# Sparse attention followed by a two-layer feed-forward: paced late loads, one more block in the seven-product form, and a re-ordered head

## Chip, cores and metric

The kernel runs on one core of a Trainium2 chip. The metric is device time in microseconds (us) of one execution; the median of three runs of the kernel before is 305.44 us (305.16 to 306.75).

## What is computed

```python
B, H, S, D = 8, 8, 576, 64
scores = q @ k.transpose / 8
mask_local   = (0 <= i - j) & (i - j < 32)          # heads 0 to 3
mask_strided = (i >= j) & (i % 32 == j % 32)        # heads 4 to 7
attn = softmax(where(mask, scores, -1e9)) @ v
x = attn laid out as [4608 tokens, 512]
h = x @ w_in                                        # 512 -> 2048
g = s * relu(h)**2 + b
out = g @ w_out                                     # 2048 -> 512, float32
```

## The kernel before, in words

Everything is in fp16 with fp32 sums. The attention of a batch is four pairs of heads: two local pairs (tiles of 96 queries against 128 keys) and two strided pairs (72 positions, 8 groups). A pair is a list of small TensorE steps: transposes of q and k, scores (L557), attention times v (L614, with a column of ones in v that gives the softmax sum), and transposes of the normalised result x (L662) into xT, where tokens lie along the free axis. For later batches the transposes of q, k and x are done by the DMA engines instead (`k_dma`, `q_dma`, `x_dma`, `x_out` with `x_in`), from the batch numbers in `QB_DMA, KB_DMA, QS_DMA, XS_DMA = 6, 4, 3, 4` on. The strided x of the last batch (7) is still transposed on TensorE.

The feed-forward runs over nine blocks T of 512 tokens. F1 (L907) makes 16 hidden tiles of 128 x 512, each of four matmuls of 512 columns; ScalarE or VectorE takes the relu, and a pair of tiles is then squared into gT. F2 multiplies gT by w_out. Blocks 0 to 2 do it plainly (`ff2`, L965): 4 token groups x 16 matmuls of 512 columns. From block `SEVEN = 3` on `ff2_seven` (L875) is used: the 2 x 2 split of the product with seven half-size products instead of eight, 112 matmuls of 256 columns. For it VectorE forms sums of the left operand (L747, eight instructions of 128 x 1024 a block) and combinations `w_mix` of the weights (L769, four instructions once, after F2 of block 2), and combines the results (L794, L806, L817) where the plain form has four evictions (L976).

The order of all instructions is written by a planner inside the kernel (`Plan`), at build time. It keeps an estimated clock, a free time for each engine and an estimated time at which each value is ready (`LAT` for latency after a queue's work, `landing(...)` and the table `AT` for loads), and emits TensorE's steps one by one: attention steps when they are ready and the attention is behind its due share (`due`), F1 and F2 steps otherwise, and filler matmuls (`keep_running`, L1201) where the first 16 F1 steps have not begun and nothing is ready. The estimates decide the order alone. On the chip each engine takes its instructions in that order and waits on semaphores, so a step that stands too early holds up all that stands behind it.

Loads of q, k, v and of the weights are issued on GpSimd's queue (POOL; the loads convert to fp16 on the way). For batch b + 2 they come in two bunches: `fetch_qk`, behind copies `gate` (L1036) that wait for the k transposes of the batch before, and `fetch_v`. From batch 4 on that is some 17 DMAs in a row. Local v of batch 0 is staged as fp32 in the space of w_out, in two halves, by SP's queue (`stage_v`, L252), and cast by GpSimd (L338). Stores of the output and all DMA transposes go through SP's queue.

At the start (the head) the order on GpSimd's queue is: q and k of batch 0, strided v, casts of v, the three loads of w_in behind a `gate` on qs (L1096), casts again, then the `second` bunch: q, k, v of batch 1 (four DMAs for local v, L316) and the four quarters of w_out (L334). AT and `landing` hold the planner's times for these.

Of the kernel before, what the change touches and what calls it, by code (L numbers as in the profile page):

```python
# [15 lines left out]
class Plan:  # L16
# [6 lines left out]

    LAT = {"A": 70.0, "V": 70.0, "P": 70.0, "D": 12000.0, "X": 7000.0, "Y": 12000.0}

# [3 lines left out]
    def __init__(self):  # L29
        self.t = 0.0  # L30
        self.done = {}
        self.pend = []
        self.free = {"A": 0.0, "V": 0.0, "P": 7000.0, "D": 0.0, "X": 0.0, "Y": 0.0}
        self.banks = {}
# [82 lines left out]
class Step:  # L117
    def __init__(self, fn, ns, needs=(), group=None, keys=(), posts=(), after=None):
        self.fn, self.ns, self.needs, self.group = fn, ns, needs, group
        self.keys, self.posts, self.after = keys, posts, after  # L120


@with_exitstack
def kernel(
# [32 lines left out]
    for p in range(SQ):  # L157
        for c in range(SQ):
# [29 lines left out]
    w_in_sb = [const.tile([128, 4, n], FP16, name=f"w_in_sb{i}")  # L188
               for i, n in enumerate((512, 512, 1024))]
    w_out_sb = const.tile([128, NFT, DM], FP16)  # L190
# [20 lines left out]
    def x_free(b):  # L211
# [21 lines left out]
    NL, NS = 4 * LT * D, 4 * ST * D  # L233
    vl_stage = w_out_sb.rearrange("p f m -> p (f m)").bitcast(FP32)[:, 0:NL].rearrange(
        "p (h t d) -> p h t d", h=4, d=D)

# [33 lines left out]
    for tl in p_bufs[False]:  # L270
        nc.vector.memset(tl[:, 16 * SQ:], 0.0)

    nc.vector.memset(part32, 1.0 / 32)
# [39 lines left out]
    def load_vl(b):  # L313
        vl = v_loc[b % NV]
        for h in range(4):
            nc.gpsimd.dma_start(out=vl[LPAD:128, h, :, 0:D], in_=v_band(b, h))  # L316
# [8 lines left out]
    def load_w_in():  # L325
        wv = moe_w_in.rearrange("(c p) f -> p c f", p=128)
        for i, at in enumerate((0, 512, 1024)):
            nc.gpsimd.dma_start(out=w_in_sb[i], in_=wv[:, :, at:at + w_in_sb[i].shape[2]])
# [26 lines left out]
    def cast_v(b, loc, mm, key):  # L355
        nt, np_, dst = (LT, 128, v_loc) if loc else (ST, SQ, v_str)

        def g(eng):
            src = vl_stage if loc else loaded[b, "vs"].rearrange(
                "p (h t d) -> p h t d", h=4, d=D)  # L360
            for h in range(2 * mm, 2 * mm + 2):
                copy_on(eng, out=dst[b % NV][0:np_, h, :, 0:D], in_=src[:, h])
        n = nt * D
        plan.post([key], {"P": 1000.0} if loc else {"A": 2 * (170 + 0.83 * n), "V": 540.0,
                                                           **({"P": 1500.0} if b == 0 else {})}, g,
                  [("cast", b, mm) if loc else ("in", "vs", b, mm)])
        if loc:
            rows_before(b, mm, ("cast", b, mm))

    def rows_before(b, mm, key):  # L370

        hs = slice(2 * mm, 2 * mm + 2)
        vl = v_loc[b % NV]
        src = vl_stage[:, :, :, 0:D] if b == 0 else vl[:, :, :, 0:D]

        def g(eng):
            copy_on(eng, out=vl[0:LPAD, hs, 1:LT, 0:D], in_=src[128 - LPAD:128, hs, 0:LT - 1])
        plan.post([key], {"P": 800.0} if b == 0 else {"A": 700.0, "V": 350.0}, g, [("in", "vl", b, mm)])

# [29 lines left out]
    def pair_steps(b, m):  # L409
# [10 lines left out]
        def trans(name, j, group):  # L420
            alone = loc and b < HEAD_T

            def f():
                if j == 0:
                    st["p" + name] = bank(group).bitcast(FP16)[:, 0:S]
                if alone:
                    for e in range(2):
# [11 lines left out]
                    rhs=ident[0:nq, 0:nq], is_transpose=True)  # L439
            s = Step(f, 70 if alone else 35, needs=[("in", name + sfx, b, mm)],  # L440
                     group=group if j == 0 else None)
            if j == nt - 1:
                key = ("t", name, id_)
# [33 lines left out]
        q_by_dma = b >= (QB_DMA if loc else QS_DMA)  # L477
        x_by_dma = b >= 2 if loc else XS_DMA <= b < B - 1

# [234 lines left out]
    SQ_ACT = 0  # L714
    SEVEN = 3
    H = NFT // 2
# [44 lines left out]
    def mix_post():  # L761

        wl, wr = [[w_out_sb[:, H * j:H * j + H, 256 * k:256 * k + 256] for j in range(2)]
                  for k in range(2)]
        jobs = ((3, wr[1], wr[0]), (1, wr[0], wl[0]), (2, wr[1], w_mix[1]), (4, wl[1], w_mix[2]))
        before = [("F2", SEVEN - 1)]
        for i, x, y in jobs:
            plan.post(before, {"V": 1250.0},
                      lambda eng, i=i, x=x, y=y: nc.vector.tensor_tensor(  # L769
                          out=w_mix[i], in0=x, in1=y, op=ALU.subtract), [("w_mix", i)])  # L770
            before = [("w_mix", i)]
        plan.post([("ev", SEVEN - 1, ts) for ts in range(4)], {"V": 350.0},
                  lambda eng: nc.vector.tensor_tensor(
                      out=bcs[:, 256:512], in0=bcs[:, 256:512], in1=bcs[:, 0:256],
                      op=ALU.subtract), [("dbc",)])
# [121 lines left out]
    def ff1(T, ft, ct, group, cts=(0, 1, 2, 3), early=False):  # L897
        tok0 = T * PS
        def f():
# [6 lines left out]
            for lo, hi in ((0, n), (n, PS))[:1 + (n < PS)]:  # L906
                nc.tensor.matmul(  # L907
                    out=gts["h", T, ft][:, lo:hi],
                    lhsT=w_in_sb[min(ft // 4, 2)][:, ct].rearrange(
                        "p (c x l) -> p c l x", x=128, l=4)[:, max(ft // 4 - 2, 0), ft % 4],  # L910
                    rhs=xT[ct][:, (at + lo) % (NX * S):(at + lo) % (NX * S) + hi - lo],
                    start=(ct == cts[0] and lo == 0), stop=(ct == cts[-1] and hi == PS))
# [109 lines left out]
    def landing(cost):  # L1022

        nonlocal ring
        ring = max(ring, plan.t + 2000.0) + cost

        return ring + (6000.0 if plan.t > 60000.0 else 600.0)

# [3 lines left out]
    def fetch_qk(b):  # L1032
# [6 lines left out]
        for name in ("q", "k"):  # L1039
# [3 lines left out]
            if b < HEAD_T:  # L1043
                arrive(both(name + "l", b), landing(1500))
                continue
            plan.done["raw", name, b] = landing(1700 if b > 1 else 1450)
            for mm in range(2):
                pair_post(b, name, mm, ("raw", name, b))
        for name in ("qs", "ks"):
            arrive(both(name, b), landing(2000 if b > 1 else 1750))  # L1050

# [11 lines left out]
    def early_v(b):  # L1063

        loaded[b, "vs"] = inp.tile([SQ, NS], FP16, tag="vs", name="vs")
        load_s(loaded[b, "vs"], v, b)
        plan.done["raw", "v", False, b] = landing(1800)
        for mm in range(2):
            cast_v(b, False, mm, ("raw", "v", False, b))

    gate = const.tile([64, 4], FP16)

    def after_landing(i, src):

        nc.sync.dma_start(out=gate[0:1, i:i + 1], in_=src)

    load_qk(0)
    early_v(0)
    plan.free["P"] = 7100.0
    plan.free["V"] = 6500.0  # L1080
    AT = {"ql0": 5700.0, "kl0": 6800.0, "ql1": 7900.0, "kl1": 8900.0, "qs": 10100.0,
          "ks": 11600.0, "vs": 13600.0, "vl0": 7100.0, "vl1": 14700.0}
    for key, at in AT.items():
# [4 lines left out]
    after_landing(0, loaded[0, "ql"][0:1, NL // 2:NL // 2 + 1])  # L1088
    stage_v(range(2, 4))
    nc.sync.dma_start(out=masks, in_=h_mask.ap())  # L1090
    nc.sync.dma_start(out=s_sb, in_=moe_s.to_broadcast([128, 1]))
    nc.sync.dma_start(out=b_sb, in_=moe_b.to_broadcast([128, 1]))
    def weights_in(eng):

        nonlocal ring
        nc.gpsimd.tensor_copy(out=gate[0:8, 2:3], in_=loaded[0, "qs"][64:SQ, 0:1])  # L1096
        load_w_in()
        ring = 15300.0
        for keys, cost in ([0], 2700), ([1], 2500), ([2, 3], 5000):
            arrive([("w_in", c) for c in keys], landing(cost))  # L1100

    for mm, at in (0, AT["vl0"]), (1, AT["vl1"]):
        plan.done["raw", "v", True, 0, mm] = at
        cast_v(0, True, mm, ("raw", "v", True, 0, mm))
    plan.post([("in", "vl", 0, 0)] + both("qs", 0), {"P": 2500.0}, weights_in, [("w",)])
# [6 lines left out]
    def second(eng):  # L1112

        fetch_qk(1)
        load_vl(1)
        plan.done["raw", "vl", 1] = landing(3200)
        for mm in range(2):
# [3 lines left out]

    plan.post(both("vl", 0) + both("vs", 0) + [("w",)], {"P": 14000.0}, second, [("free",)])

# [11 lines left out]
    for b in range(B):  # L1135
        for m in range(4):
            steps, last_av = pair_steps(b, m)
            att.append(steps)
            if b + 2 < B:

                if m == 0:
                    plan.post(
                        [("fetch_v", b + 1) if b else ("free",)] +
                        [("q", (b, mk)) for mk in range(4)] + [("k", (b, mk)) for mk in range(4)] +
                        [("soon" if b > 1 else "k", (b + 1 if b > 1 else b, mk)) for mk in range(2, 4)],
                        {"P": 2900.0 + (2200.0 if b + 2 >= QB_DMA else 0.0)},
                        lambda eng, b=b: fetch_qk(b + 2), [("fetch", b + 2)])
                last_av.after = when_all("av", b, lambda b=b: plan.post(
                    [("fetch", b + 2)] + both("vs", b), {"P": 3600.0}, lambda eng: fetch_v(b + 2),
                    [("fetch_v", b + 2)]))  # L1150

    f1, f2 = [], []
    for T in range(NBLK):
# [26 lines left out]
        for ts in range(4):  # L1180

            parts = 2 if T == NBLK - 1 and ts == 3 else 1
            for part in range(parts):
                gr = Group("f2", F2B)
                for ft in range(NFT):
                    f2.append(ff2(T, ts, ft, gr, part, parts))
                    f2[-1].pos = T + 0.25 + (ts + (part + ft / NFT) / parts) / 4
    def keep_running(until):

        ghz = 1.2 if plan.t < 6000 else 2.4  # L1190
        n = min(int((until - 100.0 - plan.t) * ghz) - 20, 512) // 128
# [25 lines left out]
    while i2 < len(f2) or any(at_i[p] < len(att[p]) for p in range(len(att))):  # L1217
# [4 lines left out]

        active = [p for p in range(first, min(first + 4, len(att))) if at_i[p] < len(att[p])]
        for p in active:
            r = plan.step_ready(att[p][at_i[p]])
# [66 lines left out]
```

## Time and profile before

| | |
|---|---|
| median of 3 runs | 305.44 us |
| the profiled execution, its own time | 306.2 us |
| its span, first to last instruction | 304.4 us |
| TensorE (PE) busy, first matmul, start of the last matmul | 296.4 us, 1.05 us, 300.97 us |
| VectorE (DVE), ScalarE (ACT), GpSimd (POOL) busy | 216.6, 183.9, 99.3 us |
| granted TensorE clock | 1.000 |
| q0, GpSimd's DMA queue | 57232 packets, 18.08 MB |
| q1, SP's DMA queue | 43562 packets, 18.78 MB |

A busy PE is not a PE at its peak: the ends of pipelined matmuls are modelled, so a matmul of 512 columns is listed with 379 ns while the next one starts some 216 ns after it. The pace is therefore read from pieces of the chain of work (so many matmuls in so many microseconds), not from the mean of one. In the waits, the columns are the total, the number of times and the longest, in microseconds. A GpSimd DMA row gives the time of the issuing instruction; its landing comes later.

### The profile page before, as it was taken

How to read it: one execution, taken by the hardware profiler on the slowest of the kernel's cores; microseconds unless marked ns; L12 is line 12 of the kernel's file. 1: busy time of each engine (PE TensorE's matmuls, PEld its weight loads, DVE VectorE, ACT ScalarE, POOL GpSimd, SP SyncE). 2: the span in 40 equal slices, each digit the busy share in tenths (PEclk: the TensorE clock that was granted, in tenths of full speed). 3: DMA queues.
4: the chain of work that ended last, by engine and by line, in shares of the span. 5: the costliest groups of instructions: out<-in, count | busy, mean ns of one | idle time of the engine just before them, and what ended most of it. 6: DMA issues, size and time to landing. Idle time of an engine off the chain costs nothing.

```text
span 304.4 us, 6800 instructions
## 1 busy us (share of the span) xinstructions
PE 296.4 (97%) x2674; PEld 205.8 (68%) x2674; DVE 216.6 (71%) x474; ACT 183.9 (60%) x330; POOL 99.3 (33%) x146
## 2 busy tenths in 40 slices
PE   8998999999999999999999999999999999999995
PEld 3764655666555568767567776778888666766784
DVE  6665897698966688737997698777765366737563
ACT  2966963898747677478585946695725445445300
POOL 8771753930961095029502961200000000000000
PEclk9999999999999999999999999999999999999999
DMA  8999999999999699999999999944010200300123
GB/s 136 183 201 202 137 213 190 179 198 149 83 160 165 98 100 149 132 186 147 142 153 172 142 160 159 155 105 131 14 37 34 72 34 0 106 0 2 69 82 126
DMA packets 100826, 37.29 MB, mean 122 GB/s; under 512 B 80907, under 2 KB 97803, under 8 KB 100795
## 3 DMA queue, kind: packets, MB, share of 16 engines
q0 software_dynamic: 57232, 18.08, 60.1%
q1 hardware_dynamic: 43562, 18.78, 33.3%
q8 instruction: 21, 0.34, 0.5%
q14 instruction: 11, 0.08, 0.1%
HBM read 36.86 MB, written 10.32 MB: 155 GB/s over the span
## 4 chain that ended last, share of the span: by engine, by line
PE 83%; DMA 8%; DVE 3%; POOL 3%; issue 1%; ACT 1%; POOLq 0%
PE ps_f L907 36%; PE ps_f L875 20%; PE ps_f L965 12%; DMA kl<-in_k_dram 5%; PE ps_s L557 3%; PE ps_a L614 3%; DMA vs<-in_v_dram 2%; PE ps_s L875 2%; DMA xT<-x_dram 1%; PE ps_t L875 1%; PE ps_s L965 1%; PE ps_t L614 1%; PE ps_t L662 1%; PE ps_t L437 1%; PE ps_f L437 1%
## 5 line engine op out<-in xcount | busy, mean ns | idle before, releaser
L907 PE MATMUL ps_f<-xT,w_in_sb 128*128 128x512 f16 (+4 forms) x696 | 148.1, 340 | 0.0
L934 ACT ACTIVATE u<-ps_f 128x512 f16<-128x512 f32 x137 | 80.8, 595 | 72.6 <-PE ps_f L907 69.9
L907 PEld LDWEIGHTS <-w_in_sb 128*128 128x128 f16 x704 | 71.7, 113 | 33.1 <-DMA w_in_sb<-in_moe_w_in_dram 0.5
L875 PEld LDWEIGHTS <-gT 128*128 128x128 f16 x512 | 49.0, 98 | 12.5 <-issue 0.4
L965 PE MATMUL ps_f<-w_out_sb,gT 128*128 128x512 f16 x176 | 47.6, 379 | 0.0
L875 PE MATMUL ps_f<-w_out_sb,gT 128*128 128x256 f16 x312 | 44.2, 273 | 0.3 <-DVE o L806 0.3
L944 DVE TENSOR_TENSOR gT<-u 128x1024 f16<-128x1024 f16 x46 | 32.1, 697 | 15.1 <-ACT u L934 14.4
L942 ACT ACTIVATE gT<-u 128x1024 f16<-128x1024 f16 x26 | 27.5, 1057 | 0.7
L640 DVE TENSOR_TENSOR x_nat<-ps_a,rec 72x256 f16<-72x256 f32 (+1 forms) x55 | 25.3, 459 | 0.9
L316 POOL DMA_DIRECT2D v_loc<-in_v_dram x28 | 20.7, 759 | 14.3 <-DMA w_in_sb<-in_moe_w_in_dram 6.0
L965 PEld LDWEIGHTS <-gT 128*128 128x128 f16 x192 | 17.0, 98 | 11.1
L575 ACT ACTIVATE p_str<-ps_s 72x432 f16<-72x432 f32 (+1 forms) x45 | 20.1, 481 | 4.7 <-PE ps_s L557 4.6
L575 ACT ACTIVATE p_loc<-ps_s 128x384 f16<-128x384 f32 x46 | 20.8, 494 | 2.2 <-PE ps_s L557 1.8
L614 PEld LDWEIGHTS <-p_str 72*128 72x128 f16 x256 | 15.3, 98 | 7.3 <-issue 0.4
L747 DVE TENSOR_TENSOR gT<-gT 128x1024 f16<-128x1024 f16 x28 | 18.5, 683 | 1.4 <-ACT gT L942 1.3
L875 PE MATMUL ps_f<-w_mix,gT 128*128 128x256 f16 x144 | 19.3, 273 | 0.0
L875 PEld LDWEIGHTS <-S 128*128 128x128 f16 x160 | 15.5, 98 | 3.7
L629 DVE RECIPROCAL rec<-ps_a 72x4 f32<-72x4 f32 (+1 forms) x55 | 9.7, 177 | 11.2 <-PE ps_a L614 11.0
L321 POOL DMA_DIRECT2D v_str<-in_v_dram x16 | 13.0, 816 | 9.6 <-PE ps_f L907 5.6
L583 DVE TENSOR_TENSOR p_loc<-p_loc,masks 128x1152 f16<-128x1152 f16 x14 | 10.5, 750 | 7.6 <-ACT p_loc L575 7.4
L875 PE MATMUL ps_f<-w_mix,S 128*128 128x256 f16 x96 | 13.4, 273 | 0.0
L976 DVE SCALAR_TENSOR_TENSOR o<-ps_f,s_sb,bcs 128x512 f32<-128x512 f32 x11 | 8.2, 749 | 6.4 <-PE ps_f L965 6.2
(162 smaller groups left out, 413.2 us busy)
## 6 DMA issues: line engine op xcount, KB each, us to landing
out_dram<-o SPq DMA_DIRECT2D x34, 256.0 KB, 3.4
w_out_sb<-in_moe_w_out_dram POOLq DMA_DIRECT2D x4, 512.0 KB, 9.4
v_loc<-in_v_dram POOLq DMA_DIRECT2D x28, 72.0 KB, 8.5
qs<-in_q_dram POOLq DMA_DIRECT2D x6, 288.0 KB, 6.6
ks<-in_k_dram POOLq DMA_DIRECT2D x6, 288.0 KB, 8.0
ql<-in_q_dram POOLq DMA_DIRECT2D x5, 288.0 KB, 9.7
kl<-in_k_dram POOLq DMA_DIRECT2D x16, 72.0 KB, 3.8
v_str<-in_v_dram POOLq DMA_DIRECT2D x16, 72.0 KB, 9.9
```

What stands on the lines that cost most here:

```text
L316: nc.gpsimd.dma_start(out=vl[LPAD:128, h, :, 0:D], in_=v_band(b, h))
L321: nc.gpsimd.dma_start(out=vs[:, h, :, 0:D], in_=v[b, 4 + h].rearrange("(p j) d -> p j d", j=ST))
L575: nc.scalar.activation(out=st["pw", g][0:nk, 0:2 * n * nq], in_=st["s", g][0:nk, 0:2 * n * nq], func=AF.Exp, scale=scale)
L614: nc.tensor.matmul(out=st["a"][:, j % per, :], lhsT=st["pw", g][0:nk, i * nq:i * nq + WIDE], rhs=vt[0:nk, 2 * mm + e, j, :])
L640: nc.vector.tensor_tensor(out=st["x"][:, j0:j0 + per, 64 * e:64 * e + 64], in0=st["pa", e, j][0:nq, 0:per, 0:D], in1=st["rec", e, j][0:nq, ...
L747: nc.vector.tensor_tensor(out=at(out), in0=at(x), in1=at(y), op=op)
L875: nc.tensor.matmul(out=gts[name, T, t][:, 0] if halves else gts[name, T][:, t], lhsT=lhs(k, t), rhs=rhs(k), start=fresh and k == 0 and (ha ...
L907: nc.tensor.matmul(out=gts["h", T, ft][:, lo:hi], lhsT=w_in_sb[min(ft // 4, 2)][:, ct].rearrange("p (c x l) -> p c l x", x=128, l=4)[:, ma ...
L934: nc.scalar.activation(out=u, in_=gts["h", T, ft], func=AF.Relu)
L942: nc.scalar.activation(out=g, in_=u, func=AF.Square)
L944: nc.vector.tensor_tensor(out=g, in0=u, in1=u, op=ALU.mult)
L965: nc.tensor.matmul(out=gts[id_], lhsT=gts[T][:, ft, ts * 128:(ts + 1) * 128], rhs=w_out_sb[:, ft, cols], start=(ft == 0), stop=(ft == NFT ...
```

## The change

Five things change together.

1. `SEVEN` goes from 3 to 2, so block 2 uses `ff2_seven`. The weight combinations are made in another order: 3, 2 and 4 after F2 of block 0 and the bias row, 1 (which overwrites a quarter of w_out) after F2 of block 1.
2. From batch 4 on the loads go out by turns: up to four DMAs per turn, one turn for each pair of hidden tiles that is squared (`in_turn`, with a GpSimd copy `gate` that reads that pair of gT).
3. The strided x of batch 7 is transposed by DMA too (`x_by_dma`).
4. Local v of batch 1 is one DMA of 96 x 24 x 64 instead of four; the second half of local v of batch 0 comes by a DMA on GpSimd's queue straight into its place, ahead of strided v, instead of through SP's queue and a cast.
5. The head: w_in is loaded in four parts of 512 columns instead of 512, 512 and 1024; the planner's landing times change; its clock starts at 1850 ns; transposes of batch 0 that have begun go first (`sticky`). In the order as built 8 filler matmuls of 512 columns stand before the first transpose of q where 13 stood, and ahead of the first transpose of k of batch 1 stand 42 F1 matmuls where 38 stood. The planner's latencies for DMA transposes and for the way of x through memory are lowered.

```diff
-    LAT = {"A": 70.0, "V": 70.0, "P": 70.0, "D": 12000.0, "X": 7000.0, "Y": 12000.0}
+    LAT = {"A": 70.0, "V": 70.0, "P": 70.0, "D": 6000.0, "X": 5000.0, "Y": 5000.0, "Z": 0.0}
...
-               for i, n in enumerate((512, 512, 1024))]
+               for i, n in enumerate((512, 512, 512, 512))]
...
     def load_vl(b):
         vl = v_loc[b % NV]
+        if b < 2:
+            nc.gpsimd.dma_start(
+                out=vl.rearrange("p h t d -> p (h t) d")[LPAD:128, :, 0:D],
+                in_=v.rearrange("b h (t p) d -> b p (h t) d", p=LQ)[b, :, 0:4 * LT])
+            return
         for h in range(4):
...
-        x_by_dma = b >= 2 if loc else XS_DMA <= b < B - 1
+        x_by_dma = b >= 2 if loc else XS_DMA <= b
...
-    SEVEN = 3
+    SEVEN = 2
...
-        jobs = ((3, wr[1], wr[0]), (1, wr[0], wl[0]), (2, wr[1], w_mix[1]), (4, wl[1], w_mix[2]))
-        before = [("F2", SEVEN - 1)]
+        early = [("bcs",)] + ([("F2", SEVEN - 2)] if SEVEN > 1 else [])
+        jobs = ((3, wr[1], wr[0], ALU.subtract, early), (2, w_mix[3], wl[0], ALU.add, []),
+                (4, wl[1], w_mix[2], ALU.subtract, []),
+                (1, wr[0], wl[0], ALU.subtract, [("F2", SEVEN - 1)]))
...
-        return ring + (6000.0 if plan.t > 60000.0 else 600.0)
+        return ring + (4000.0 if plan.t > 60000.0 else 600.0)
...
+    SPREAD, PER, LATE = 4, 4, 5000.0
+    turn = [0, 0]
+
+    def in_turn(fns, needs=()):
+
+        if turn[0] <= i1 // 8:
+            turn[0], turn[1] = i1 // 8 + 1, 0
+        for fn, keys in fns:
+            T, at = turn[0] // 8, turn[0] % 8
+            key = ("g", T, ff_order(T)[2 * at]) if T < NBLK else None
+
+            def go(eng, fn=fn, key=key, first=turn[1] == 0):
+                if first and key:
+                    nc.gpsimd.tensor_copy(out=gate[0:1, 0:1], in_=gts[key[1]][0:1, key[2], 0:1])
+                fn()
+            plan.post(list(needs) + [key] * (key is not None), {"P": 760.0}, go, keys, LATE)
+            turn[1] += 1
+            if turn[1] == PER:
+                turn[0], turn[1] = turn[0] + 1, 0
...
     load_qk(0)
+    nc.gpsimd.dma_start(
+        out=v_loc[0].rearrange("p h t d -> p (h t) d")[LPAD:128, 2 * LT:4 * LT, 0:D],
+        in_=v.rearrange("b h (t p) d -> b p (h t) d", p=LQ)[0, :, 2 * LT:4 * LT])
     early_v(0)
...
-    stage_v(range(2, 4))
...
+    plan.t = 1850.0
+
...
+        active.sort(key=lambda p: not att[p][at_i[p]].sticky)
```

`spread_qk` and `spread_v` hand the loads of a batch to `in_turn`: q local, k local, q strided, k strided (behind the same two `gate` copies as before), then local v and strided v, a head at a time. They take the place of `fetch_qk` and `fetch_v` where b + 2 >= SPREAD.

## The prediction on record

> **What bounds the kernel now.** I read the engine totals first, then PE's own waits, then the chain that ended last for PE's pace, and only then GpSimd's queue.
>
> ```profile
> PE 296.4 (97%) x2674; PEld 205.8 (68%) x2674; DVE 216.6 (71%) x474; ACT 183.9 (60%) x330; POOL 99.3 (33%) x146
> ```
>
> PE is occupied nearly throughout; every other engine has room on average. All that PE waited for after its start:
>
> ```profile
> PE ps_t L429 <- DMA ql<-in_q_dram: 1.4, 1, 1.4
> ...
> PE ps_t L429 <- DMA kl<-in_k_dram: 0.6, 1, 0.6
> PE ps_s L557 <- ACT kT_loc L338: 0.4, 1, 0.4
> PE ps_s L907 <- DMA w_in_sb<-in_moe_w_in_dram: 0.4, 1, 0.4
> PE ps_f L875 <- DVE o L806: 0.3, 1, 0.3
> ```
>
> With one more of 0.2 us on x these are all. They are a few tenths to 1.4 us each, and the DMA ones lie in the head: w_in at 18.9 us, ql of batch 1 at 28.5 us, kl of batch 1 at 31.2 us (start times of the matmuls behind them). From 35 us on PE runs at its pace to the end; there only fewer or cheaper matmuls shorten the kernel, and any new wait lengthens it. The pace comes from the chain of work (start, length, what):
>
> ```profile
> 17.06 14.12 DMA kl<-in_k_dram
> ...
> 82.27 1.95 PE ps_f L965 x9
> ...
> 233.11 4.04 PE ps_f L875 x37
> ```
>
> A 512-column matmul costs 1.95 / 9 = 216.7 ns, a 256-column one 4.04 / 37 = 109.2 ns. The first line says that the head's end is set by kl of batch 1, issued at 17.06 us and landed 14.1 us later behind everything on that queue. GpSimd's rows (start, length of the issue, idle time before and what ended it) show why:
>
> ```profile
> 22.06 0.75 POOL L316 DMA_DIRECT2D v_loc<-in_v_dram  x1 [1.96 <-DMA w_in_sb<-in_moe_w_in_dram]
> 26.89 0.72 POOL L316 DMA_DIRECT2D v_loc<-in_v_dram  x1 [4.08 <-DMA w_in_sb<-in_moe_w_in_dram]
> 28.73 0.73 POOL L316 DMA_DIRECT2D v_loc<-in_v_dram  x1 [1.11 <-DMA ql<-in_q_dram]
> 31.47 0.72 POOL L316 DMA_DIRECT2D v_loc<-in_v_dram  x1 [2.01 <-DMA kl<-in_k_dram]
> ...
> 33.63 2.15 POOL L334 DMA_DIRECT2D w_out_sb<-in_moe_w_out_dram  x4
> ```
>
> The last row is the issue of w_out behind them. Each of the four v issues waits for the DMA issued eight before it, and the data come in order of issue. The whole queue is limited by its rate there, not by when POOL issues.
>
> **What the skill says.** "TensorE: Matmul & The Clock Gate", section "Back-to-back issue gap": about N / 2.4 + 2.5 ns, so 215.8 and 109.2 ns; the two paces above agree. The same page, Part 1, says the clock doubles after about 3.4 us of sustained matmuls in a window that runs freely. Here the fillers start 427 ns apart until 5.72 us and at full pace from there, after 4.7 us; the page fits. "DMA: Bandwidth & Descriptors", section "Anatomy of one DMA", prices a GpSimd DMA at 2.0 us plus bytes / 436 GB/s: 2.7 us for a 288 KB ql. The trace has 4.2 to 4.4 us for the two that found the queue empty (76.1 and 107.0 us); I use the trace.
>
> **The change part by part** (against the profiled span of 304.4 us).
>
> *Seven products in block 2.* Removed 64 x 216.7 = 13.87 us, added 112 x 109.2 = 12.23 us: **-1.64 us** on PE, which is the path. VectorE gains eight sums of 683 ns (L747), seven combining evictions of 750 ns and one add of 692 ns, and loses four evictions of 749 ns: 5.46 + 5.25 + 0.69 - 3.00 = +8.4 us. The four weight combinations only move, some 60 us earlier. Two windows (us, us, then busy of PE, PEld, DVE, ACT, POOL):
>
> ```profile
> 100.00:130.00 30.00, 30.00 (x283) 20.47 (x282) 23.45 (x60) 19.72 (x37) 11.88 (x19) 1.00 1.27 124
> ...
> 170.00:180.00 10.00, 9.69 (x103) 7.85 (x101) 9.83 (x22) 5.73 (x12) 9.56 (x13) 1.00 1.88 134
> ```
>
> Block 2's second product stands between about 100 and 140 us. With 8.4 us more VectorE would be asked for 31.9 of 30 us, so the planner must put squares on ScalarE (1057 ns there against 697), which has 10 us free. The second window is what a full VectorE does to PE: 9.83 of 10 us busy, and PE lost 0.3 to 0.5 us. The cost lies between 0 (the sums are spread over 40 us and ScalarE takes the rest) and 2 us (four such stalls). I take **+0.5 us**.
>
> *x of batch 7 by DMA.* 16 transposes of 72 columns go, at 33 ns each (eight alike take 0.26 us at 12.6 us): **-0.53 us**. Two copies on ScalarE and VectorE go too, hidden. SP gets two stores and two transposes more; queued behind them are stores of the output, which have no reader. Who waits is F1 of block 7: as built, 14.6 us of matmuls stand between the last attention product and its first matmul, against a sum of about 0.2 + 0.5 (rec, x) + two ways of 0.5 + 3.3 and 1.2 + 3.3 us = 9 us. So 0, and a stall only if SP is held for over 5 us there.
>
> *Head.* I take the landing times of w_in, ql and kl as unchanged: the same bytes are ahead of them, since the v half that moves to POOL's queue left SP's queue on the same engines. Its 1152 packets of 128 bytes need about 1.5 to 2 us (549 to 773 such packets per us at 30 to 32 us), as the fp32 ones of SP's did at 12 to 14 us. PE waits for ql until 28.5 us as before and begins F1 at 29.1 us; ten F1 matmuls instead of six then take 2.17 us, to 31.3 us, where kl has just landed (31.2 us). Four matmuls are moved into the old wait: 4 x 216.7 - 60 = **-0.8 us**. Bounds: if kl lands 1 us later or earlier, +0.2 to -1.0. That q can start earlier than at 6.4 us (it landed by 5.2 us: issue at 1.27, 3.9 us to landing) is worth nothing, because F1 waits for w_in at 18.9 us anyhow. Fewer fillers leave PE idle for about 0.8 us before q; if the clock came up later for it, the small matmuls up to 9 or 12 us would run at half pace. Up to about 2 us of that are covered by the waits at 18.9 and 28.5 us; without this cover it is 1 to 3 us. I take 0.
>
> *One transfer for v of batch 1, w_in in four.* POOL saves four waits (1.96 + 4.08 + 1.11 + 2.01 = 9.2 us) and two issues; w_out is issued at about 31 instead of 33.6 us, behind kl's landing. PE did not wait for w_out before, and its first use moves up by only 0.5 us. So 0; if the single transfer needs a far emptier queue, w_out comes later, up to +1.5 us.
>
> *Late loads by turns.* POOL is 33% busy; a gate copy is 0.18 us plus its wait, some 18 of them, and behind each wait stand only loads, the two k gates and one or two casts. PE waited for no late load before, so **0** is to be gained. What shrinks is the lead. As built, 17 us of matmuls stand between the first turn of batch 7 and its first score. It takes four issues (3.0 us), a landing (4.1 us for a single load; 8 to 11 us in the old bunches), SP's issue (1.8 us), the transpose (4.4 to 8.9 us) and the spreading copies (1.5 us): 14.8 to 19.3 us. Pacing should keep the queue short, which speaks for the low end. Bounds 0 to +6 us; I take 0.
>
> Sum: -1.64 - 0.53 - 0.8 + 0.5 = **-2.5 us**. The profiled execution took 306.2 us (span 304.4 plus 1.8), which would become 303.7; it lies 0.8 us above the median of 305.44, so against the median I say **303.0 us**.
>
> **The rivals.**
>
> *A, the forecast*: 301.8 to 304.0 us, likeliest 303.0; chance 0.50. For it: PE's pace is even, the removed matmuls lie on it.
>
> *B, more is gained*: VectorE costs nothing and the queue, free of POOL's waits, delivers kl and w_out earlier: 305.4 - 3.0 - 1.0 = 301.4 us; chance 0.10. Against it: the head's rate is that of the queue.
>
> *C, the gain is paid back in small stalls* at 100 to 200 us: 2 us for VectorE's share, or one or two late transposes of 1 us: 304.5 to 306 us; chance 0.24. It is also the case that the form of block 2 is no gain once VectorE is full.
>
> *D, slower*: the shortened lead. Transposes of q and k still take 8.9 us, as qTl did at 150 and 180 us, because a transpose now always meets loads on the same engines. Then 19.3 us are needed where 17 stand, PE's queue holds the score in front of ready F1 work, and each pair waits about 1.5 to 2.3 us, two waits in each of batches 5, 6 and 7: about +5.5 us, 305.4 - 2.5 + 5.5 = 308.4 us. It decides from a transpose of about 6.6 us on (17 - 14.8 + 4.4). Chance 0.16. For it: 8.9 us in the trace, and lowered latencies in the planner. Against it: alone they take 2.7 to 4.4 us.
>
> **How the numbers follow.** About 0.5% (1.5 us) is what a measurement of this kernel tells from no change, so faster means under 303.9 us. Nearly all of A and B lies there: 0.58. Same: C and the upper rim of A, 0.26. Slower, over 307.0 us: D, 0.16. The range from 300.8 to 306.6 us holds A, B and C and leaves out D.
>
> **What would show it.** Right: 112 more L875 matmuls at 109 ns and 64 fewer 512-column ones; the wait for kl gone, that for ql still there; PE's waits after 35 us under 1 us in total; w_out issued near 31 us. Wrong: waits of the scores for DMA kT or for copies of qT after 100 us (D); waits of the seven-product matmuls for VectorE (C); fillers and transposes at the 427 ns pace beyond 6 us, with F1 starting later than 19 us (the clock); F1 of block 7 waiting for DMA xT.

## The result: 12% slower, and the profile after

The changed kernel takes 342.53 us (median of 4 runs, 340.29 to 345.2) where the kernel before, on the same chip, takes 306.09 us: ratio 1.120, 95% interval 1.111 to 1.129. The forecast was 303.0 us with a range up to 306.6. Rival D (the shortened lead of the late loads) had the side right and the size wrong, 308.4 us.

The profiled execution took 342.33 us, its span is 340.6 us, and the granted clock of TensorE fell from 1.000 to 0.965. Its engine totals:

```profile
PE 304.7 (89%) x2706; PEld 214.3 (63%) x2706; DVE 217.6 (64%) x486; ACT 190.6 (56%) x335; POOL 99.8 (29%) x157
```

No engine has become a bound. The work is nearly that of before, and every engine's share is lower, so the added time is waiting. PE's own waits say for what (columns: total, times, longest):

```profile
PE ps_s L565 <- DMA kT_alt<-kl: 6.3, 2, 5.0
PE ps_f L622 <- POOL v_str L345: 6.1, 1, 6.1
PE ps_s L565 <- DMA kT_loc<-kl: 5.7, 1, 5.7
PE ps_a L622 <- DVE x_nat L648: 4.8, 1, 4.8
PE ps_s L565 <- ACT p_loc L583: 2.8, 1, 2.8
PE ps_s L565 <- DMA kT<-ks: 2.0, 1, 2.0
```

Before, the longest wait was 1.4 us, and none over 0.3 us came after 35 us. The list of matmuls gives the account. The columns of all matmuls, at the N / 2.4 ns of the prediction's formula, sum to 286.5 us before and 283.7 after, so the change did take 2.8 us of work off PE (0.6 of it fillers). What passes between the starts of matmuls beyond that, called holes here, grew by 38.2 us, from 13.4 to 51.6. Of these, 29.0 us are seven holes of 1.5 to 6.3 us, at 44, 118, 155, 158, 165, 193 and 233 us. Another 7.9 us are matmuls at half clock after the long ones; the page's row of granted clock (40 slices of 8.5 us, in tenths) shows where:

```profile
PEclk9999978999999969999999959999899999999999
```

The low digits follow the waits at 44 us (7 and 8), 118 us (6), 193 us (5) and 233 us (8). The shorter waits at 155 to 165 us (1.5, 3.0 and 2.2 us) left no mark.

*Three kinds of wait.* The first is in the head. GpSimd's rows (start, length, idle time before and what ended it), then PE's:

```profile
47.60 0.72 POOL L323 DMA_DIRECT2D v_loc<-in_v_dram  x1 [1.92 <-DMA w_out_sb<-in_moe_w_out_dram]
49.13 0.73 POOL L313 DMA_DIRECT2D vs<-in_v_dram  x1 [0.81 <-DMA ql<-in_q_dram]
49.91 1.17 POOL L345 COPY v_str<-vs 72x512 f16<-72x512 f16 x2
```

```profile
50.58 0.38 PE L622 MATMUL ps_f<-v_str,p_str 72*128 72x65 f16 x4 [6.13 <-POOL v_str L345]
```

The cast of strided v of batch 1 is now given to POOL. It stands behind the issues of batch 2's loads, and each of those waits for an earlier DMA. PE's queue holds the product that needs it.

The second kind is a late v, with VectorE between. VectorE's row, and PE's:

```profile
121.94 0.33 DVE L345 COPY v_loc<-v_loc 32x640 f16<-32x640 f16 x1 [5.62 <-DMA v_loc<-in_v_dram]
```

```profile
123.46 0.38 PE L622 MATMUL ps_a<-v_str,p_str 72*128 72x65 f16 x4 [4.78 <-DVE x_nat L648]
```

PE waits for x_nat, which has nothing to do with the late v of batch 4: it is only queued behind the copy that does. In all, VectorE waited 25.2 us for v_loc (0.2 us before). The third kind is the scores' wait for transposed k, the one that the forecast had asked about.

Why are the data late? GpSimd's rows for the first gate of each of batches 4 to 7:

```profile
104.16 0.18 POOL L1096 COPY gate<-gT 1x1 f16<-1x1 f16 x1 [25.05 <-DVE gT L954]
...
139.50 0.18 POOL L1096 COPY gate<-gT 1x1 f16<-1x1 f16 x1 [20.37 <-ACT gT L952]
...
175.13 0.18 POOL L1096 COPY gate<-gT 1x1 f16<-1x1 f16 x1 [21.62 <-DVE gT L954]
...
215.12 0.18 POOL L1096 COPY gate<-gT 1x1 f16<-1x1 f16 x1 [22.32 <-DVE gT L954]
```

A turn opens with a pair of squares, and squares belong to the first product alone. Between the last square of one block and the first of the next none came for 9.6 to 14.4 us (89.7 to 104.1, 125.4 to 135.0, 161.6 to 173.0 and 198.8 to 210.2 us). POOL stands still longer, for 20 to 25 us. Only batch 4 waits for the first pair of a block. The first gates of batches 5, 6 and 7 open with the third, second and third pair of theirs: `in_turn` names the pair after the one that the planned order has reached when the loads are allowed, and by then that is well inside the next first product. Then a batch's loads go out at one per 0.9 to 1.0 us, as dense as the bunches were (0.9 to 1.1). Issue of the first q load and start of the first local scores of the same batch, in us:

| batch | before: load, scores, between | after: load, scores, between |
|---|---|---|
| 4 | 76.1, 108.1, 32.0 | 104.7, 125.8, 21.1 |
| 5 | 107.0, 136.9, 29.9 | 140.0, 156.6, 16.6 |
| 6 | 135.4, 167.6, 32.2 | 175.6, 199.4, 23.8 |
| 7 | 166.9, 197.5, 30.6 | 215.6, 238.1, 22.5 |

*As forecast.* The wait for kl of batch 1 is gone, that for ql is left (0.9 us), and w_out is issued near 31 us:

```profile
24.14 1.19 POOL L318 DMA_DIRECT2D v_loc<-in_v_dram  x1 [2.27 <-DMA w_in_sb<-in_moe_w_in_dram]
...
30.83 0.56 POOL L341 DMA_DIRECT2D w_out_sb<-in_moe_w_out_dram  x1 [1.84 <-DMA kl<-in_k_dram]
```

The pace at the end is the old one, 8 matmuls of 512 columns in 1.73 us. The two windows that the prediction showed are now:

```profile
100.00:130.00 30.00, 25.22 (x184) 14.39 (x182) 17.97 (x42) 17.15 (x32) 14.24 (x22) 0.89 1.26 110
...
170.00:180.00 10.00, 10.00 (x91) 6.49 (x89) 8.28 (x25) 7.84 (x12) 4.56 (x7) 1.00 0.82 86
```

In the first, PE is busy for 25.2 of 30 us at a clock of 0.89, and VectorE, feared to be full, for only 18.0. With PE waiting that says little of the fear; experiment 9 does.

### The profile page after: what moved, and what is told of

Its sections match the earlier page's. It is cut to its first block, busy times and chain, and to the rows that moved or that the text cites. A ratio compares the mean times of both kernels' runs of the same rounds, so it can differ in the third digit from the quotient of the medians.

```text
span 340.6 us, 6910 instructions
## 1 busy us (share of the span) xinstructions
PE 304.7 (89%) x2706; PEld 214.3 (63%) x2706; DVE 217.6 (64%) x486; ACT 190.6 (56%) x335; POOL 99.8 (29%) x157
## 4 chain that ended last, share of the span: by engine, by line
PE 59%; DMA 19%; issue 9%; POOL 5%; SPq 3%; DVE 1%; ACT 1%; POOLq 0%; DVEq 0%
PE ps_f L918 25%; PE ps_f L886 17%; DMA kT<-ks 5%; DMA ql<-in_q_dram 4%; DMA kT_loc<-kl 4%; PE ps_s L565 3%; DMA kT_alt<-kl 3%; PE ps_f L975 3%; DMA v_loc<-in_v_dram 2%; PE ps_s L886 2%; SPq L524 1%; DMA kl<-in_k_dram 1%; PE ps_a L622 1%; POOL kl L1111 1%; PE ps_t L886 1%
## 5 line engine op out<-in xcount | busy, mean ns | idle before, releaser
L886 PEld LDWEIGHTS <-gT 128*128 128x128 f16 x608 | 59.4, 100 | 14.7 <-issue 0.9
L886 PE MATMUL ps_f<-w_out_sb,gT 128*128 128x256 f16 x376 | 55.8, 279 | 0.1
L975 PE MATMUL ps_f<-w_out_sb,gT 128*128 128x512 f16 x112 | 32.5, 406 | 0.0
L1096 POOL COPY gate<-gT 1x1 f16<-1x1 f16 x18 | 4.2, 233 | 89.5 <-DVE gT L954 69.0
L886 PE MATMUL ps_f<-w_mix,gT 128*128 128x256 f16 x176 | 24.3, 279 | 0.5 <-DVE Vb L805 0.5
L755 DVE TENSOR_TENSOR gT<-gT 128x1024 f16<-128x1024 f16 x34 | 22.7, 678 | 1.4 <-ACT gT L952 1.3
L345 ACT COPY xT<-ps_t 128x576 f16<-128x576 f16 x7 | 4.5, 636 | 27.6 <-PE ps_t L670 26.0
L345 DVE COPY v_loc<-v_loc 32x640 f16<-32x640 f16 x9 | 2.8, 324 | 25.2 <-DMA v_loc<-in_v_dram 25.2
L565 PE MATMUL ps_s<-qD_loc,kT_loc 128*128 128x192 f16 x68 | 12.8, 276 | 5.7 <-DMA kT_loc<-kl 5.7
L975 PEld LDWEIGHTS <-gT 128*128 128x128 f16 x128 | 11.9, 102 | 9.4 <-issue 1.4
L886 PE MATMUL ps_f<-w_mix,S 128*128 128x256 f16 x112 | 15.8, 273 | 0.0
```

Source lines behind the costliest of these rows:

```text
L565: nc.tensor.matmul(out=st["s", g][0:nk, c:c + 2 * nq], lhsT=(st["k"][:, i * nq:i * nq + nk] if loc else st["k"][:, i, 0:SQ]), rhs=st["q"][ ...
L755: nc.vector.tensor_tensor(out=at(out), in0=at(x), in1=at(y), op=op)
L886: nc.tensor.matmul(out=gts[name, T, t][:, 0] if halves else gts[name, T][:, t], lhsT=lhs(k, t), rhs=rhs(k), start=fresh and k == 0 and (ha ...
L975: nc.tensor.matmul(out=gts[id_], lhsT=gts[T][:, ft, ts * 128:(ts + 1) * 128], rhs=w_out_sb[:, ft, cols], start=(ft == 0), stop=(ft == NFT ...
```

## The experiments

Four theories were set against each other. T1: the planner was told landings that are too short. T2: the pacing itself brings the data too late. T3: the cast on POOL costs its wait. T4: block 2's new form or the head stall by themselves. Times are medians; the kernel before took 305.7 to 306.2 us beside these, and ratios are to it.

**1. The planner's landings put back, turns kept.** For T1: the planner believes that a late load takes 5 us and a transpose 5 to 6, and so queues VectorE's copies and PE's scores too early.

```diff
-    LAT = {..., "D": 6000.0, "X": 5000.0, "Y": 5000.0, ...}
+    LAT = {..., "D": 12000.0, "X": 7000.0, "Y": 12000.0, ...}
-        return ring + (4000.0 if plan.t > 60000.0 else 600.0)
+        return ring + (6000.0 if plan.t > 60000.0 else 600.0)
-    SPREAD, PER, LATE = 4, 4, 5000.0
+    SPREAD, PER, LATE = 4, 4, 14000.0
```

> The changed kernel (342.5 us) with one thing put back: what the planner assumes for a late load and for a transpose by DMA (late load 14 us in place of 5, transposes 12/7/12 us in place of 6/5/5, landing surcharge 6 us in place of 4). The late loads still go out by turns, four per pair of squares. Theory T1 (the planner was told too short landings, so VectorE, ScalarE and TensorE were given work in order whose data had not come): the waits of 2.0 to 6.3 us after 100 us go, about 24 us, and some 4 us of slow clock after them; only the 6.1 us at 44 us stays: 310 to 316 us. Theory T2 (the pacing itself brings the data too late, whatever the planner believes): the waits change their name and stay as long, 335 to 345 us, since the planner then has squares it may not start and fills nothing.

Measured: 353.2 us, ratio 1.155 (1.148 to 1.161): slower still, and above both forecasts. T1 as the only cause fell. VectorE's waits for late v went from 25.2 to 0.3 us, so the belief does make those; but the time didn't come back. GpSimd's first gates in this kernel:

```profile
105.31 0.18 POOL L1096 COPY gate<-gT 1x1 f16<-1x1 f16 x1 [41.97 <-ACT gT L952]
...
145.11 0.84 POOL L1096 COPY gate<-gT 1x1 f16<-1x1 f16 x1 [25.12 <-ACT gT L952]
...
179.55 0.57 POOL L1096 COPY gate<-gT 1x1 f16<-1x1 f16 x1 [27.34 <-DVE gT L954]
...
232.34 0.63 POOL L1096 COPY gate<-gT 1x1 f16<-1x1 f16 x1 [31.79 <-DVE gT L954]
```

POOL stands longer. The gates lie 35 to 40 us apart in the changed kernel and 34 to 53 us here, while the bunches of before came every 28 to 32 us. I read a loop in this: a batch's loads wait for a first product, the batch's attention waits for the loads, and a later first product waits for that attention. A planner that allows longer for the landing would make the loop longer. That is a reading of the gates' times; no run tests the loop by itself.

**2. Bunches, short landings kept.**

```diff
-    SPREAD, PER, LATE = 4, 4, 5000.0
+    SPREAD, PER, LATE = 8, 4, 5000.0
```

> The changed kernel with the late loads in bunches again (as soon as their buffers are free, not four per pair of squares), and the short assumed landings kept for the transposes (6/5/5 us). T2 (pacing is the cause): the late stalls go with the pacing, 312 to 318 us, and the loads of batches 4 to 7 go out near 76, 107, 135 and 167 us as in the kernel before. T1 (short assumed landings are the cause): transposes by DMA still take 7 to 11 us against 5 to 6 assumed, so the waits of scores for kT and kT_alt stay, 2 to 6 us each, though those of VectorE for v fall: 322 to 332 us.

Measured: 317.7 us, ratio 1.039 (1.031 to 1.046). Without turns 25 us come back, as T2 said. The loads of batches 4 to 7 go out from 84, 109, 135 and 168 us. PE's longest waits left:

```profile
PE ps_f L622 <- POOL v_str L345: 6.5, 1, 6.5
PE ps_f L918 <- ACT u L944: 2.6, 1, 2.6
PE ps_s L565 <- DMA kT_alt<-kl: 2.1, 1, 2.1
```

**3. The cast of batch 1 kept off POOL, all else as changed.**

```diff
-                             **({"P": 1250.0} if b < 2 else {})}, g,
+                             **({"P": 1250.0} if b < 1 else {})}, g,
```

> The changed kernel with the cast of the strided v of batch 1 kept off POOL (the planner may choose VectorE or ScalarE, as before the change). T3 (the POOL cast stands behind batch 2's load issues, which wait for DMA slots, and costs its 6.1 us wait and 1 to 2 us of slow clock): 334 to 337 us, the gap at 44 us gone. Rival: the wait only moves to the load of that v or to the next late operand in the head, and less than 3 us are gained: 339.5 to 343 us.

Measured: 344.7 us, ratio 1.127 (1.119 to 1.134): nothing gained, less than even the rival allowed. The wait itself is gone. One window of the changed kernel and then of this one (us, length, busy of PE, PEld, DVE, ACT, POOL, clock):

```profile
38.00:52.00 14.00, 7.87 (x78) 4.81 (x76) 7.11 (x18) 5.42 (x12) 8.80 (x11) 0.82 1.33 199
```

```profile
38.00:52.00 14.00, 12.91 (x148) 7.29 (x146) 12.12 (x35) 8.18 (x16) 7.29 (x9) 1.00 1.26 203
```

The first gate opens at 99.8 us, 4.4 us earlier than in the changed kernel, the second at 139.6 against 139.5: the lead is gone within one block, in which PE now waits 6.3 us for x_nat. A hole ahead of a slower stage is worth nothing until that stage is mended.

**4. All three put back: bunches, long landings, no POOL cast** (the edits of 1 and 3, with SPREAD 8; LATE, which only turns use, then plays no part).

> The changed kernel with three things put back at once: late loads in bunches, the long assumed landings, and the cast of batch 1 off POOL. What is left of the change is the seven-product form from the third block, x of batch 7 by DMA, the reordered head and the single transfer of v of band two with w_in in four. If T1, T2 and T3 together are the whole loss, this ends where the prediction put the rest, 301 to 305 us (kernel before 306.1). If the seven-product form in block 2 crowds VectorE or the new head stalls by itself (rival T4), it ends at 308 to 320 us with waits in the stretch of block 2 (95 to 140 us) or ahead of 45 us.

Measured: 307.9 us, ratio 1.0059 (1.0033 to 1.0085). Of the 36 us lost, 35 lie in these three edits. The 2.5 us that the rest was to gain are not there.

**5. Turns without the gate.** The order by turns, the short landings and the POOL cast stay; a turn waits for no square.

```diff
-            key = ("g", T, ff_order(T)[2 * at]) if T < NBLK else None
+            key = None
```

> The changed kernel with one thing taken away: a turn of late loads waits for no square (the copy into gate ahead of each four, and the turn's due step, are left out). The order of the loads by turns, the short assumed landings and the POOL cast stay. T2, sharpened (a turn waits for a square of the next first product, so the loads of a batch stand still through the second product, 20 to 25 us, and come about 28 us later than in bunches): the loads of batch 4 go out near 76 to 90 us again and the kernel ends like the one with bunches, 315 to 321 us. Rival (the queueing order or the flat cost of 5 us that the planner puts on a late load is what hurts): 330 us or more.

Measured: 332.4 us, ratio 1.087 (1.080 to 1.093). Batch 4's loads start at 80.5 us, as T2 said, and those of batches 5 to 7 at 101.3, 135.2 and 165.4 us, which is 24 to 50 us ahead of the changed kernel. But only 10 us came back, which is the rival's number. What PE waited for:

```profile
PE ps_t L622 <- DVE x_nat L648: 8.3, 2, 4.4
PE ps_f L622 <- POOL v_str L345: 6.6, 1, 6.6
```

So either the queue by turns is bad in itself or the short landings are. The next kernel was made for that.

**6. No gate, and long landings** (the edits of 5 and 1).

> The kernel without the gate (332.4) with the long assumed landings put back (14 us for a late load, 12/7/12 us for transposes, 6 us surcharge). The gate is gone, so the data can come in time; if what is left over bunches is the planner's belief (T1, now as a second cause), the waits of VectorE for x_nat and v and of TensorE behind them go and it ends like bunches with long landings, 314 to 319 us. If it is the queue form itself (18 POOL instructions of 760 ns each planned one by one, loads that wait in POOL's order for buffers still in use, casts of q behind them), it stays at 325 us or more with waits of POOL's v_str loads for the products of the batch before.

Measured: 315.5 us, ratio 1.029 (1.021 to 1.037). It was the landings. PE's longest waits are now the cast, and after it 2.3 us in all:

```profile
PE ps_f L622 <- POOL v_str L345: 6.6, 1, 6.6
PE ps_f L886 <- DVE Va L805: 2.3, 3, 1.0
```

The queue by turns costs nothing once the gate is away and the planner knows the landings.

**7. Bunches and long landings, POOL cast kept** (prices the cast).

> Bunches and long assumed landings put back in the changed kernel, the POOL cast of batch 1 left as changed. Against bunches alone (317.7) this gives the short landings their price, against all three put back (307.9) it gives the cast its price. T3: the cast costs its wait of 6.5 us and a little slow clock with nothing later to give it back to: 314 to 316 us, so the leads are worth 2 to 4. Rival: the cast's wait is hidden once the leads are long (its needs come earlier in the plan): 308 to 311 us, and the leads are worth most of the 10.

Measured: 315.3 us, ratio 1.031 (1.024 to 1.037), and without the cast it was 307.9: the cast costs 7.5 us, a wait of 6.6 us and the slow clock behind it. It is not hidden by longer leads. Its row on PE here:

```profile
51.61 0.38 PE L622 MATMUL ps_f<-v_str,p_str 72*128 72x65 f16 x4 [6.58 <-POOL v_str L345]
```

In kernel 4 VectorE does this cast among others at 38.8 us.

**8. One wait per batch: 18 loads a turn in place of 4.**

```diff
-    SPREAD, PER, LATE = 4, 4, 5000.0
+    SPREAD, PER, LATE = 4, 18, 5000.0
```

> The changed kernel with 18 late loads to a turn in place of four, so that a batch's loads wait once for a square of the next first product and then go out together. If the wait of 20 to 25 us for that first square is the loss and the pacing inside the first product does nothing (four a turn already go out at one per 0.8 us, as bunches do), this stays near the changed kernel, 335 to 350 us. If the spacing within the turns is what delays the last loads of a batch, it gains 5 to 10 us: 332 to 337 us.

Measured: 343.0 us, ratio 1.119 (1.110 to 1.128), the time of the changed kernel. The pacing inside the first product neither helps nor harms; what is left of the gate, and does the harm, is the wait for a batch's first turn.

The six kernels with the POOL cast make a table (us):

| | short landings | long landings |
|---|---|---|
| turns with gate | 342.5 | 353.2 |
| turns without gate | 332.4 | 315.5 |
| bunches | 317.7 | 315.3 |

The gate costs 10 us where the planner is too hopeful anyway, and 38 us where it is not. The hopeful landings cost 17 us without the gate, about 2 us with bunches (which have their own, less hopeful, estimate; two runs each, whose intervals overlap), and with the gate they even gain 11.

**9. The seven-product form in block 2 alone,** on the kernel before.

```diff
-    SEVEN = 3
+    SEVEN = 2
```

(with the changed order of the weight combinations)

> The kernel before with the seven-product form from the third block alone (with its reordered mixes of w_out), nothing else. The prediction's term: 1.64 us less on TensorE and 0.5 back for VectorE, about 304.6 us, ratio 0.996. Rival T4 (block 2's VectorE has no room and the second product waits for its sums): 306 to 308 us, with new waits of the second product for Va, Vb, Ua or w_mix between 120 and 155 us.

Measured: 305.6 us, ratio 0.9985 (0.9962 to 1.0007). In the profiled execution PE's columns fell by 1.70 us and its holes grew by 1.61 us. One window where it is lost, and PE's row there:

```profile
140.00:150.00 10.00, 9.29 (x106) 8.47 (x105) 9.96 (x23) 5.04 (x11) 7.89 (x11) 1.00 1.84 157
```

```profile
149.82 1.91 PE L878 MATMUL ps_f<-w_out_sb,gT 128*128 128x256 f16 x16 [0.71 <-DVE Va L797]
```

VectorE is busy for 9.96 of 10 us, and the second product waits for one of its results. That is less than half of it. As much goes near 195 us, where the scores wait for transposed k (1.0 us in two waits, none before):

```profile
195.56 0.50 PE L557 MATMUL ps_s<-qD_loc,kT_alt 128*128 128x192 f16 x4 [0.73 <-DMA kT_alt<-kl]
```

**10. The head alone** (kernel 4 with SEVEN and x of batch 7 as before).

> The kernel before with the head alone: second band v in one transfer, w_in in four parts, v of batch 0 by two ways, the assumed times of the head; bunches, long landings and the cast choice as before; no seven-product in block 2 and no x of batch 7 by DMA. The prediction's term: 0.8 us less, 305 us. Since all parts but pacing, leads and cast gave 307.9 against 305.7 where 303 was forecast, the rival has the head losing: 307 to 309 us, with the 1 to 2 us lying ahead of 45 us in the gaps between matmuls.

Measured: 307.1 us, ratio 1.0033 (1.0014 to 1.0051): a loss of about 1 us in place of a gain of 0.8. Two new waits on PE stand out:

```profile
5.50 0.45 PE L436 MATMUL ps_t<-ident,ql 96*64 96x96 f16 x12 [1.28 <-DMA ql<-in_q_dram]
```

```profile
41.27 0.36 PE L622 MATMUL ps_f<-v_loc,p_loc 128*128 128x65 f16 x6 [1.06 <-DVE p_loc L591]
```

The first cost nothing: the first product starts at 18.60 us here, at 18.97 before. Nothing covers the second. Counted in columns without fillers, PE had done 28.2 us of work at 40 us where it had done 27.1 before, and 28.9 against 29.0 at 42 us. So in this execution the head did gain its time, 1.2 us, and this wait took it back. What else is in the 0.9 us that the medians lose stays open.

**11. x of batch 7 by DMA alone.**

```diff
-        x_by_dma = b >= 2 if loc else XS_DMA <= b < B - 1
+        x_by_dma = b >= 2 if loc else XS_DMA <= b
```

> The kernel before with the strided x of batch 7 transposed by DMA alone. The prediction's term: 0.53 us less on TensorE, nothing lost: ratio 0.998, 305.6 us. Rival: four more transposes on SP's queue near 210 us delay the last first product's x and cost up to 1 us: ratio 1.000 to 1.003.

Measured: 307.2 us, ratio 1.0041 (1.0017 to 1.0064). In the profiled execution PE's columns fell by 0.48 us and its last matmul starts 0.3 us earlier, with one new wait at 238 us:

```profile
238.21 1.47 PE L875 MATMUL ps_f<-w_out_sb,gT 128*128 128x256 f16 x12 [0.84 <-DVE Va L794]
```

The trace doesn't show where the median's 1.3 us lie. It isn't the clock: the nine executions at a granted clock of 1.000 have a median of 307.3 us, the 24 such ones of the kernel before 305.6. This stays open.

**12. Both parts that take work off PE, nothing else** (9 and 11 on the kernel before).

> The kernel before with the seven-product form from the third block and x of batch 7 by DMA, the two parts of the change that take work off TensorE. If they add: ratio 0.9965 (the 0.6 us measured for the first and 0.5 for the second), about 305 us, the version that beats both kernels. If the stalls for Va near 149 us and for kT_alt near 195 us that ate the first part's gain grow with the four transposes more: ratio 0.999 to 1.003.

Measured: 305.1 us, ratio 0.9971 (0.9951 to 0.9991). It is under the kernel before by 0.9 us by the ratio, 0.7 by the medians. The columns fall by 2.18 us (1.70 + 0.48), the holes grow by 0.55. The parts don't add (0.9985 and 1.0041 would give 1.0026). I take it that each edit makes the planner deal out a new order, and that the small waits of that order are worth as much as the edits; no run shows this.

## Why the prediction was wrong, point by point

- **Late loads by turns, "I take 0", bounds 0 to +6: this step failed.** Its parts:
  - "PE waited for no late load before, so 0 is to be gained. What shrinks is the lead." This was right, and is rival D.
  - The lead was taken from the order as built for batch 7 alone: 17 us of matmuls stood there, 14.8 to 19.3 us were thought to be needed. The chip took 16.6 to 23.8 us from the first load to the scores, in all four batches.
  - "Pacing should keep the queue short" was wrong. Turns open only in the first product, where loads go out as densely as in bunches (one per 0.9 to 1.0 us). v_str took a median of 13.7 us from issue to landing (9.9 before), and q's transposes 7.1 us (3.2 before).
  - The sum held only the way of k. It left out v: its landing (8.9 us in the median, 13.8 at most), its copy on VectorE, and all that VectorE had queued behind the copy. Experiment 1 shows that this, with 25.2 us, came from the planner's new landings.
  - That no turn can open in a second product can be read in the diff (the key is a square of gT). The prediction named "its wait" and what stands behind it, but didn't ask how long the wait lasts: POOL stands for 20 to 25 us ahead of each batch's first turn, 9.6 to 14.4 of them without any square. Experiments 5, 6 and 8 show that the harm comes from this gate and not from the pacing inside the first product.
- **The cast of batch 1 was not costed at all.** The edit (POOL as a choice while b < 2) is one condition in the diff of the kernels, and the account of the change above leaves it out. It is worth 7.5 us (experiment 7), and GpSimd's order behind w_out has the waiting loads ahead of it.
- **Seven products in block 2:** -1.64 us on PE was right (1.70 us of columns). The term "+0.5 us" for VectorE was too small: the holes grew by 1.6 us in the trace, and by the medians about 1.0 of the 1.64 us was lost again. Both lie inside its bounds of 0 to 2, but only 0.7 us is the named wait for VectorE; 1.0 us is waiting for transposed k.
- **x of batch 7:** -0.53 us on PE was right (0.48); alone it gave no gain.
- **The head:** the new order and w_out's issue came as forecast, the -0.8 us didn't last. Alone the head cost 0.9 us by the medians: in the profiled execution it was 1.2 us ahead at 40 us and lost that to a wait of 1.1 us for p_loc at 41 us that no step asked about (experiment 10).

*The clock in the head* was asked about, and its sign of being wrong came in the changed kernel. Twelve transposes that took 0.45 us before take 0.69, up to 11 us:

```profile
7.18 0.45 PE L429 MATMUL ps_a<-ident,kl 96*64 96x96 f16 x12
```

```profile
6.96 0.69 PE L436 MATMUL ps_a<-ident,kl 96*64 96x96 f16 x12
...
10.99 0.69 PE L436 MATMUL ps_f<-ident,kl 96*64 96x96 f16 x12
```

Full clock comes at 12.8 us (6.0 before), and the first product starts at 19.81 us (18.97 before). The granted clock of 0.965 doesn't hold this, since the record of the clock begins only at 12.8 us; the pace shows it. By 35 us PE had done as much work as before (22.4 and 22.3 us of columns), so the later waits covered the delay, as the prediction allowed; but in experiment 10, with less half clock in the head, it was 1.2 us ahead there. It varies: of the ten profiled executions with the new head three had full clock by 5.7 us and kept it through the head, and seven had it to keep only from 9.8 to 13.2 us on, while all four with the old head had it by 6.6 us (one lost it for 3.4 us at 18.9).

*The clock after long waits* was not asked about. The Trainium skill, "TensorE: Matmul & The Clock Gate", Part 1, has it fall back to half after an idle window of about 3.4 us. In the changed kernel the waits of 4.8 to 6.1 us were followed by slow stretches, those of 2.8 us and less were not. But in experiment 3 a wait of 2.2 us was enough. Two windows of that kernel, PE's row there, and two windows around the changed kernel's wait of 2.8 us (the hole of 3.0 us at 158 us; the clock is the third number from the end):

```profile
163.44:166.85 3.41, 1.23 (x18) 0.74 (x17) 2.65 (x8) 1.77 (x3) 0.00 (x0) 1.00 1.18 274
166.85:170.26 3.41, 3.41 (x13) 1.80 (x13) 0.11 (x1) 1.75 (x4) 0.00 (x0) 0.50 0.44 121
```

```profile
166.84 1.87 PE L918 MATMUL ps_f<-xT,w_in_sb 128*128 128x512 f16 x4 [2.18 <-DMA xT<-x_dram]
```

```profile
156.14:159.55 3.41, 1.91 (x17) 1.63 (x18) 0.75 (x1) 2.38 (x4) 0.00 (x0) 1.00 2.60 107
159.55:162.97 3.42, 1.65 (x18) 1.54 (x18) 2.00 (x4) 3.32 (x8) 0.00 (x0) 1.00 1.65 164
```

In every trace here the changes of the clock lie whole multiples of 3.41 us apart. The 2.2 us fell into one such stretch and left PE busy for 1.23 us of it; the longer wait was split over two. So the measurement differs from a plain limit of 3.4 us on the wait: where a wait falls counts too, and no run shows where the limit lies. A long wait here costs more than its length: the cast 7.5 us for a wait of 6.6 us.

Against the sum: the parts other than turns, landings and cast were to give -2.5 us and gave +1.8 (experiment 4); turns, landings and cast were put at 0 and gave 35 us. The first group missed by 4.3 us, and the second alone moves the result to the slow side. Rival D had part of the mechanism, the wait of the scores for transposed k, at the difference of two leads, without VectorE's queue and without the clock. Its sum doesn't follow from its own figures either: two waits of 1.5 to 2.3 us in each of three batches are 9 to 14 us, not 5.5.

## What to carry to other kernels

If transfers are paced by a step of the work, ask in which stretches that step doesn't occur: there the transfers stand still, and if the step depends on their data the pacing can become a loop. A planner's latency estimates belong to the change as much as its instructions: an in-order engine that is told too early a landing holds up work that has nothing to do with the late data. Cost every edit of a diff, a one-digit one too, by who stands ahead of it in its queue; and mend the stage that sets the pace before a hole ahead of it (experiments 3 and 7: the same edit is worth nothing and 7.5 us).

## What the runs showed of the hardware that I had not expected

A wait of 2.2 us could bring PE's clock down (experiment 3, 166.8 us) and one of 2.8 us leave it up (the changed kernel, 161.3 us), as it fell on stretches of 3.41 us. With the new head, which has five fillers fewer, full clock came to stay only at 9.8 to 13.2 us in seven of ten profiled executions. DMA transposes issued among dense loads took longer than others: in the medians 7.1 us for q in the changed kernel, 3.2 us before, and 2.9 us in experiment 1, where the loads landed faster too (v_str 6.8 us against 13.7). GpSimd issued the 15 late loads of batch 4 at one per 1.1 us in a bunch (before, 76.1 to 91.5 us) and at one per 1.0 us by turns (after, 104.7 to 118.3 us): four per turn spread nothing.
